# A Fourier layer and a gated feed-forward network in fp32 on one core: the first tile's down projection in plain form, and stored weights loaded from HBM by GpSimd's queue instead of SyncE's

## The chip, the cores and the metric

The kernel runs on one core of a Trainium2 chip. The metric is the device time of one execution in microseconds (us). The engines are named as in the profile: PE (TensorE, matmul), PEld (its weight loads, which overlap the matmuls), DVE (VectorE), ACT (ScalarE), POOL (GpSimd) and SP (SyncE, which here only issues DMAs; "SPq" is its DMA queue in the trace). PSUM is the memory that matmuls accumulate in, SBUF the memory of all other operands.

## What is computed

```python
def attention(x, w_r, w_i, b_r, b_i):            # x: 8 x 3008 x 256, float32
    X = np.fft.rfft(x, axis=1)
    Yr = X.real @ w_r - X.imag @ w_i + b_r
    Yi = X.real @ w_i + X.imag @ w_r + b_i
    Yr = np.sign(Yr) * np.maximum(np.abs(Yr) - 0.01, 0.0)
    Yi = np.sign(Yi) * np.maximum(np.abs(Yi) - 0.01, 0.0)
    return np.fft.irfft(Yr + 1j * Yi, n=3008, axis=1)

def moe(x, w_in, w_out):                          # 24064 x 256, 256 x 2048, 2048 x 256
    h = x @ w_in
    g = h * (1.0 / (1.0 + np.exp(-1.702 * h)))
    return g @ w_out
```

The result is `moe(attention(x))` with the batches laid end to end as 24064 tokens. `w_in` and `w_out` come as float64.

## The kernel before, in words

**Numbers.** A float32 product is made of three matmuls in the fast format fp32r (`mm3`, L136): each operand is split into a rounded part `hi` and the rest `lo`, and hi·hi, hi·lo and lo·hi are added up in PSUM. A split (`split`, L133; both lines show as L134 in the profile) is a cast on ACT, which makes `hi`, and a subtraction on DVE, which makes `lo`. The float64 weights are taken apart by integer operations (`from_float64`, L182 to L210): POOL issues the DMA of the raw words (`wraw`), ACT and DVE convert them.

**Two halves of the work.** The Fourier layer goes batch by batch. Stage A (tiles `xr`, `xh`, `aev`) contracts over 47, writes to DRAM, stage B (`br`, `kr`, `co`) contracts over 64, the mix (`mv`, then `yr` by four DMAs, L384) multiplies by the weights and applies the threshold, the inverse (`yh`, `iev`) writes `s2` to DRAM, and the last stage, `tokens`, reads that (`ur`) and fills a tile `y` of 1024 tokens for the network. The gated network goes tile by tile, 23.5 tiles of 1024 tokens, and each tile in 8 steps (q = 0 to 7) of 256 of the 2048 hidden columns. A program order written out in the main loop (L729 to L798) mixes the pieces of both; a scheduler then orders each engine's instructions from it.

**Up projection of a step.** It is a 2x2 block product done with seven products instead of eight (Strassen's scheme in Winograd's form, products 1 to 7, 3 matmuls each). It needs the weight blocks added up in a certain way, "turned". `turn_weights(0, q, ...)` (L226) does that for `w_in`. The turned weights come as two tiles, `wu` (4 products, 512 KB) and `wv` (3 products, 384 KB). The seven operands of the tile's tokens (`tk`) are split once for each tile.

**Down projection of a step.** Each step leaves four blocks of g, named (f, n). In steps 4 to 7 (`plain`, L625) a block is split (tile `gl`) and multiplied by two blocks of `wo_h` and `wo_l`, which stay in SBUF: 8 products, 24 matmuls. Steps 0 to 3 of each tile are "fast" (`NF = 4`, L32): their down projection uses the seven-product scheme too, with turned weights `wd` (4 products) and `we` (3 products). Four of the seven products are done at once (12 matmuls); the operands of the other three are kept in buffers `df` (12 of them) and multiplied in steps 4 to 7 (`solo`, L622, 9 matmuls), so that these have 33. Between the two, after step 3, `turn` (L506) combines the four PSUM banks of the tile: four copies on ACT, four additions on DVE. For a fast step `block` (L550) forms the operands with four additions and subtractions on DVE more (L564 to L572). The PSUM banks of the down projection are the tiles `po`, all others `pa`.

**Who casts g.** ACT casts blocks (0,0) and (0,1) and the fast operands; POOL casts (1,1) and (1,0) of the plain steps (`SPARE`, L461) and the three solo operands of steps 4 to 7 (`parts(..., True)`, L478).

**Turned weights in HBM.** They are made once, during tile 0, and written to HBM (`keep_turned`, L257, tiles `kept_u`, `kept_v`, `kept_d`, `kept_e`). All later tiles load them again: `load_turned` (L266) takes a new buffer and issues the load on SP's queue, 556 loads in the whole run. `wu` and `wd` share 4 buffers, `wv` and `we` another 4 (`WQ`). A load has to wait until PE has done with the buffer's old contents. A queue takes its DMAs in order, so what SP has behind it waits as well: the Fourier layer's loads and stores, all of which are on SP.

**At the start.** Before tile 0's first step three blocks of `w_in` and one of `w_out` are turned (`weights`, L671) and all four plain blocks of `w_out` are converted. During tile 0 the other five blocks of `w_in` and three of `w_out` are turned beside the steps (L731 to L734).

**What paces the mixture.** In each step a `pattern` (L761) says when the products of the up projection (numbers) and the products of the last step's down projection (0) are issued. `SHARE` (L636) spreads the Fourier pieces in `queue` over the 8 steps of a tile, in proportion; `p1` says by which step a batch must be through; `need` (L785) says how far `tokens` has to be in each step.

Of the kernel before, what the change touches and what calls it, by code (L numbers as in the profile page):

```python
# [110 lines left out]
def fourier_mix_then_gated_ffn(ctx: ExitStack, tc: tile.TileContext, x, w_r, w_i, b_r, b_i, w_in, w_out, pack, kbs, out):  # L111
# [20 lines left out]

    def split(hi, lo, src):  # L133
        return nc.scalar.copy(hi, src).ins, nc.vector.tensor_tensor(lo, src, hi.bitcast(F32), ALU.subtract).ins  # L134

# [78 lines left out]

    def plain_weights(q):
        a, e = from_float64(down_rows(q), False)
        hi, lo = wo_h[:, q - NF], wo_l[:, q - NF]
        nc.scalar.copy(hi, a)
        nc.vector.tensor_tensor(a, a, hi.bitcast(F32), ALU.subtract)
        nc.vector.tensor_tensor(lo, e, a, ALU.add)  # L220
# [5 lines left out]
    def turn_weights(d, q, spare):  # L226
# [22 lines left out]
        for h, t in zip(names, w):  # L249
            to = new_turned(0, h, q)  # L250
            split(to[:, 0], to[:, 1], t[:, :len(HALVES[h])])
            fresh.append((-1 if h == "e" else q + d, h, q, to))

# [3 lines left out]
    def keep_turned(n, behind):  # L257
        for item in [item for item in fresh if item[0] <= n]:
            fresh.remove(item)
            _, h, q, t = item  # L260
            with tc.issue_after(behind):
                nc.sync.dma_start(kept[h, q], flat(t))
            if h == "e":
                del turned_w[0, h, q]

    def load_turned(h, n):  # L266
        k, q = divmod(n, NQ)
        if k < NT and (k or h == "e") and q < (NF if h in "de" else NQ):
            nc.sync.dma_start(flat(new_turned(k, h, q)), kept[h, q])

# [189 lines left out]

    SPARE = ((1, 1), (1, 0))  # L461
    FACTORS = (1, 6, 2, 5, 7, 3, 4)
# [11 lines left out]
    def parts(t, w, name, tag, bufs, spare=False):  # L474
        p = buf([128, 2, TOK], F32R, name, tag=tag, bufs=bufs)
        hi, lo = p[:, 0, :w], p[:, 1, :w]
        if spare:
            nc.gpsimd.tensor_copy(hi, t)  # L478
            nc.vector.tensor_tensor(lo, t, hi.bitcast(F32), ALU.subtract)  # L479
        else:  # L480
            split(hi, lo, t)
        return hi, lo
# [46 lines left out]
    class Step:  # L529

        def __init__(self, tile, q, prev):


            self.tile, self.q, self.w, self.fast = tile, q, tile.w, q < NF
            self.b = prev.c if prev else None
            w = {h: turned_w.pop((tile.k, h, q)) for h in "uv"}
            self.wq = {p: (w[h][:, 0, i], w[h][:, 1, i]) for h in "uv" for i, p in enumerate(HALVES[h])}
            self.s, self.f, self.g = {}, {}, {}
# [8 lines left out]
        def cut(self, name, t):  # L547
            self.g[name] = parts(t, self.w, "gl", "gl", GL, name in SPARE)

# [58 lines left out]
        def down(self):  # L608
# [10 lines left out]

            we = turned_w.pop((tile.k, "e", q - NF))  # L620

# [3 lines left out]
            def plain(g, f, n, m):  # L625
                ms = slice(128 * m, 128 * m + 128)
                mm3(tile.bank(m, n), wo_h[:, q - NF, f, ms], wo_l[:, q - NF, f, ms], *g, start=False, stop=False, more=True)

            rest = [(lambda f=f, n=n: self.g[f, n], lambda g, f=f, n=n, m=m: plain(g, f, n, m)) for f, n in BLOCKS for m in range(2)]
            a, b, c = ((lambda t=t: parts(t, self.w, "gl", "gl", GL, True), lambda g, i=i, m=m, n=n: solo(g, i, m, n)) for i, (t, m, n) in enumerate(tile.solo.pop(0)))  # L630
            return rest[:1] + [a] + rest[1:3] + [b] + rest[3:5] + [c] + rest[5:]
# [3 lines left out]
    MANY = (6,0,2,0,5,0,7,0,0,3,0,0,0,4,0,1,0,0)  # L635
    SHARE = (1.6,.3,.3,.3,.5,1.6,1.7,1.7)  # L636

# [28 lines left out]
    def fill(count):  # L666
        for _ in range(2 * count):
            if filler:
                filler.pop(0)[1]()

    def weights(i):  # L671
        with ExitStack() as held_back:

            for ins in ([evacuated[11 if i == 1 else 15]] if i < 5 else mixed) if i else ():
                held_back.enter_context(tc.issue_after(ins))
            if i < 4:
                turn_weights(*((0, 0), (1, 0), (0, 1), (0, 2))[i], False)
                keep_turned(-1, stored[15])
            else:
                plain_weights(i + NF - 4)  # L680

# [18 lines left out]
    with tc.issue_after(loaded[2]), tc.issue_after(turned[-1]):  # L700
        fill(1)
    for i in range(4 + NQ - NF):
        weights(i)
# [134 lines left out]
```

## Time and profile before

| | |
|---|---|
| time before, median of 3 runs | 2605.38 us (2602.67 to 2610.48) |
| the profiled execution | 2605.41 us, of which its span is 2603.6 |
| PE busy | 2515.9 us, 97% |
| PEld busy | 2079.5 us, 80% |
| DVE busy | 1950.3 us, 75% |
| ACT busy | 1702.2 us, 65% |
| POOL busy | 385.5 us, 15% |
| moved by DMA | 466.17 MB, mean 179 GB/s |

The engines' busy times come from one profiled execution, whose own time stands in the second row. A group of instructions is given by source line, engine, operation and tiles, `out<-in`, with its count, its busy time, the mean length of one in ns, and the idle time of the engine just before them with what ended most of it. Matmuls overlap, so a matmul lasts longer in the record than the distance from one to the next.

### The profile page before, as it was taken

How to read it: one execution, taken by the hardware profiler on the slowest of the kernel's cores; microseconds unless marked ns; L12 is line 12 of the kernel's file. 1: busy time of each engine (PE TensorE's matmuls, PEld its weight loads, DVE VectorE, ACT ScalarE, POOL GpSimd, SP SyncE). 2: the span in 40 equal slices, each digit the busy share in tenths (PEclk: the TensorE clock that was granted, in tenths of full speed). 3: DMA queues.
4: the chain of work that ended last, by engine and by line, in shares of the span. 5: the costliest groups of instructions: out<-in, count | busy, mean ns of one | idle time of the engine just before them, and what ended most of it. 6: DMA issues, size and time to landing. Idle time of an engine off the chain costs nothing.

```text
span 2603.6 us, 37610 instructions
## 1 busy us (share of the span) xinstructions
PE 2515.9 (97%) x12477; PEld 2079.5 (80%) x12477; DVE 1950.3 (75%) x3173; ACT 1702.2 (65%) x3226; POOL 385.5 (15%) x508
## 2 busy tenths in 40 slices
PE   7889989999999999999999999999999999999998
PEld 4657878888788887888878888788887878888888
DVE  5787868778678786777867877678777787687776
ACT  4676757567676676666766767667577675675565
POOL 0002011210111111112121110110211111112212
PEclk8899999999999999999999999999999999999999
DMA  8686646455575555655566545656466564654455
GB/s 247 198 274 204 207 133 190 131 182 169 165 218 156 167 187 184 192 166 160 172 209 191 175 149 185 193 179 194 140 196 216 148 196 125 192 166 144 137 163 162
DMA packets 239938, 466.17 MB, mean 179 GB/s; under 512 B 28064, under 2 KB 115488, under 8 KB 239744
## 3 DMA queue, kind: packets, MB, share of 16 engines
q1 hardware_dynamic: 237312, 455.37, 56.1%
q0 software_dynamic: 2432, 8.39, 1.1%
q8 instruction: 100, 1.64, 0.3%
q14 instruction: 94, 0.77, 0.1%
HBM read 352.50 MB, written 85.98 MB: 168 GB/s over the span
## 4 chain that ended last, share of the span: by engine, by line
PE 79%; DMA 6%; DVE 4%; ACT 4%; issue 1%; SPq 1%; POOL 0%; ACTq 0%; DVEq 0%; POOLq 0%
PE pa L137 14%; PE pa L138 13%; PE pa L139 13%; PE po L137 11%; PE po L138 11%; PE po L139 11%; PE pa L449 4%; PE pa L349 2%; DMA yr<-mv 2%; DMA xr<-in_x 2%; ACT g L555 1%; DMA wu<-kept_u 1%; SPq L384 1%; PE pa L316 1%; DVE g L554 0%
## 5 line engine op out<-in xcount | busy, mean ns | idle before, releaser
L134 DVE TENSOR_TENSOR gl<-g,gl 128x512 fp32r<-128x512 f32 (+1 forms) x576 | 395.0, 696 | 150.1 <-ACT gl L134 148.2
L134 ACT CAST gl<-g 128x512 fp32r<-128x512 f32 (+1 forms) x576 | 350.3, 618 | 46.1 <-PE po L139 17.1
L478 POOL CAST gl<-df 128x512 fp32r<-128x512 f32 (+1 forms) x288 | 227.0, 790 | 746.4 <-PE po L139 711.4
L478 POOL CAST gl<-g 128x512 fp32r<-128x512 f32 (+1 forms) x192 | 146.5, 763 | 1287.4 <-ACT g L555 1008.8
L137 PE MATMUL pa<-tk,wu 128*128 128x512 f32 (+1 forms) x768 | 311.5, 406 | 22.0 <-ACT pa L582 9.6
L138 PE MATMUL pa<-tk,wu 128*128 128x512 f32 (+1 forms) x768 | 300.5, 391 | 0.0
L139 PE MATMUL pa<-tk,wu 128*128 128x512 f32 (+1 forms) x768 | 300.0, 391 | 0.0
L138 PE MATMUL po<-gl,wo_h 128*128 128x512 f32 (+1 forms) x768 | 298.4, 389 | 0.7 <-DVE gl L134 0.7
L545 ACT COPY s<-pa 128x512 f32<-128x512 f32 (+1 forms) x385 | 216.3, 584 | 122.0 <-PE pa L139 119.0
L139 PE MATMUL po<-gl,wo_l 128*128 128x512 f32 (+1 forms) x768 | 295.5, 386 | 0.0
L137 PE MATMUL po<-gl,wo_h 128*128 128x512 f32 (+1 forms) x768 | 289.3, 392 | 4.0 <-ACT gl L134 3.8
L554 DVE TENSOR_TENSOR g<-pa,s 128x512 f32<-128x512 f32 (+1 forms) x289 | 194.7, 675 | 86.3 <-PE pa L139 73.9
L555 ACT ACTIVATE g<-g 128x512 f32<-128x512 f32 (+1 forms) x289 | 179.7, 623 | 120.3 <-DVE g L554 117.9
L137 PE MATMUL pa<-tk,wv 128*128 128x512 f32 (+1 forms) x576 | 229.8, 399 | 0.7 <-ACT s L545 0.2
L479 DVE TENSOR_TENSOR gl<-df,gl 128x512 fp32r<-128x512 f32 (+1 forms) x288 | 208.3, 725 | 21.5 <-POOL gl L478 21.5
L138 PE MATMUL pa<-tk,wv 128*128 128x512 f32 (+1 forms) x576 | 222.5, 386 | 0.0
L139 PE MATMUL pa<-tk,wv 128*128 128x512 f32 (+1 forms) x576 | 222.2, 386 | 0.0
L137 PEld LDWEIGHTS pa<-tk,wu 128*128 128x128 f32 x768 | 146.7, 191 | 66.6 <-ACT pa L582 19.3
L555 ACT ACTIVATE g<-pa 128x512 f32<-128x512 f32 (+1 forms) x287 | 171.6, 598 | 28.0 <-PE pa L139 25.4
L139 PEld LDWEIGHTS pa<-tk,wu 128*128 128x128 f32 x768 | 146.3, 190 | 31.5 <-issue 0.8
L137 PEld LDWEIGHTS po<-gl,wo_h 128*128 128x128 f32 x768 | 143.3, 189 | 33.1 <-ACT gl L134 6.8
L138 PEld LDWEIGHTS pa<-tk,wu 128*128 128x128 f32 x768 | 146.8, 191 | 27.9 <-issue 1.9
(150 smaller groups left out, 5751.2 us busy)
## 6 DMA issues: line engine op xcount, KB each, us to landing
wu<-kept_u SPq DMA_DIRECT2D x184, 512.0 KB, 4.1
wv<-kept_v SPq DMA_DIRECT2D x184, 384.0 KB, 3.5
wd<-kept_d SPq DMA_DIRECT2D x92, 512.0 KB, 4.3
we<-kept_e SPq DMA_DIRECT2D x96, 384.0 KB, 3.6
s<-aev SPq DMA_DIRECT2D x128, 192.0 KB, 2.9
br<-s SPq DMA_DIRECT2D x96, 256.0 KB, 3.5
yr<-mv SPq DMA_DIRECT2D x384, 64.0 KB, 2.1
s<-iev SPq DMA_DIRECT2D x96, 256.0 KB, 2.6
```

Of the source, the lines that this page charges most:

```text
L134: return nc.scalar.copy(hi, src).ins, nc.vector.tensor_tensor(lo, src, hi.bitcast(F32), ALU.subtract).ins
L137: nc.tensor.matmul(ps, lhsT=wh, rhs=xh, start=start, stop=False, skip_group_check=more)
L138: nc.tensor.matmul(ps, lhsT=wh, rhs=xl, start=False, stop=False, skip_group_check=more)
L139: nc.tensor.matmul(ps, lhsT=wl, rhs=xh, start=False, stop=stop, skip_group_check=more)
L316: done_a.append(nc.tensor.matmul(ps[:96], lhsT=ka32, rhs=xs.pop(q), start=True, stop=True).ins)
L349: nc.tensor.matmul(pv[:, c, :, i], lhsT=t[:, i, cs], rhs=k[:, i], start=True, stop=True)
L449: turned.append(nc.tensor.matmul(pv[:, c, 94 * j:94 * j + 94], lhsT=t[:, j, 128 * c:128 * c + 128], rhs=kz, start=True, stop=True).ins)
L478: nc.gpsimd.tensor_copy(hi, t)
L479: nc.vector.tensor_tensor(lo, t, hi.bitcast(F32), ALU.subtract)
L545: nc.scalar.copy(t, ps[:, :self.w])
L554: nc.vector.tensor_tensor(t, ps[:, :w], self.s[other], ALU.add)
L555: nc.scalar.activation(t, ps[:, :w] if other is None else t, AF.Gelu_apprx_sigmoid)
```

## The change

It has these parts; each can be found in the diff by the names given.

- **Tile 0's steps 0 to 3 become plain** (`self.fast` asks for `tile.k > 0`). Blocks 0 to 3 of `w_out` are converted in plain form too (`wo_first`), into the `df` buffers, which tile 0 no longer uses for kept operands. `turn` and the solo products of tile 0 go.
- **The weights' conversions move.** The list `FIRST` has ten conversions ahead of the first step: (0, q) turns a block of `w_in`, (1, q) converts block q of `w_out` plainly; block 7 follows in step 0. `turn_weights(1, ...)`, four blocks, now runs in steps 2 to 5 of tile 0, and all of its results are written to HBM at once.
- **Loads on GpSimd's queue** (`load_turned`: `nc.gpsimd.dma_start`). Tile 0 loads nothing any more, so there are 552.
- **Casts.** ACT casts all blocks of g; POOL keeps the solo operands, and casts them by `tensor_scalar` (times 1, plus 0) instead of `tensor_copy`.
- **Pacing.** New `SHARE`, `p1` and `need`; the pattern of a step goes by how many down products are left from the step before (4, 8 or 11).

```diff
     def split(hi, lo, src, spare=False):
+        if spare:
+            cast = nc.gpsimd.tensor_scalar(hi, src, 1.0, 0.0, ALU.mult, ALU.add)
+        else:
+            cast = nc.scalar.copy(hi, src)
...
+    def plain_weights(q, spare):
+        a, e = from_float64(down_rows(q), spare)
+        if q < NF:
+            wo_first[q] = tuple(buf([128, 2, D], F32R, "wp", tag="df", bufs=DF) for _ in range(2))
+        hi, lo = wo_first[q] if q < NF else wo[q - NF]
...
-            fresh.append((-1 if h == "e" else q + d, h, q, to))
+            fresh.append((-1 if d else q, h, q, to))
...
-            if h == "e":
+            if h in "de":
                 del turned_w[0, h, q]
...
-        if k < NT and (k or h == "e") and q < (NF if h in "de" else NQ):
-            nc.sync.dma_start(flat(new_turned(k, h, q)), kept[h, q])
+        if 0 < k < NT and q < (NF if h in "de" else NQ):
+            nc.gpsimd.dma_start(flat(new_turned(k, h, q)), kept[h, q])
...
-    SPARE = ((1, 1), (1, 0))
...
-        if spare:
-            nc.gpsimd.tensor_copy(hi, t)
-            nc.vector.tensor_tensor(lo, t, hi.bitcast(F32), ALU.subtract)
-        else:
-            split(hi, lo, t)
+        split(hi, lo, t, spare)
...
-            self.tile, self.q, self.w, self.fast = tile, q, tile.w, q < NF
+            self.tile, self.q, self.w, self.fast = tile, q, tile.w, tile.k > 0 and q < NF
...
-            self.g[name] = parts(t, self.w, "gl", "gl", GL, name in SPARE)
+            self.g[name] = parts(t, self.w, "gl", "gl", GL)
...
-            we = turned_w.pop((tile.k, "e", q - NF))
+            wh, wl = wo_first.pop(q) if q < NF else wo[q - NF]
+            we = turned_w.pop((tile.k, "e", q - NF)) if tile.solo else None
...
+            if we is None:
+                return rest
...
+    MID = (6,0,2,0,5,0,7,0,3,0,1,0,4,0,0)
-    SHARE = (1.6,.3,.3,.3,.5,1.6,1.7,1.7)
+    SHARE = (1.3,.6,.6,.6,.6,1.3,1.5,1.5)
...
+    FIRST = ((0, 0), (1, 0), (0, 1), (0, 2), (1, 1), (1, 2), (1, 3), (1, 4), (1, 5), (1, 6))
...
-            if i < 4:
-                turn_weights(*((0, 0), (1, 0), (0, 1), (0, 2))[i], False)
-                keep_turned(-1, stored[15])
-            else:
-                plain_weights(i + NF - 4)
+            down, q = FIRST[i]
+            (plain_weights if down else lambda *at: turn_weights(0, *at))(q, False)
...
-        if n < NF - 1:
-            turn_weights(1, n + 1, True)
         if n < NQ - 3:
             turn_weights(0, n + 3, True)
+        if n + 7 < NQ:
+            plain_weights(n + 7, True)
+        if 2 <= n < NF + 2:
+            turn_weights(1, n - 2, True)
...
-            p1 = NQ * S * (nextb - 1) // TILE - 9
-        pattern = FEW if 1 <= q <= NF else MANY
+            p1 = NQ * S * (nextb - 1) // TILE - 11
+        pattern = {4: FEW, 8: MID, 11: MANY}.get(len(behind), MID)
...
-            need = TILE * (k + 1) + TILE * min(1.0, max(0.0, (part - NQ * k - 4) / 2.9))
+            need = TILE * (k + 1) + TILE * min(1.0, max(0.0, (part - NQ * k - 2) / 4.9))
...
-        if q == NF - 1:
+        if step.fast and q == NF - 1:
             closing = cur.turn
```

How this moves instructions shows at three places. Line numbers in the rows of the changed kernel are its own, four to nine higher than those of the kernel before. First DVE in tile 0's first step. Before, the sums (L554) and the fast operands (L564 to L572) stand between the `lo` parts of g (L134 with `gl`), with the turning of a block of weights (L242 and on) behind them:

```order
L554 TENSOR_TENSOR df<-pa,s 128x512
L554 TENSOR_TENSOR g<-pa,s 128x512
L564 TENSOR_TENSOR g<-g 128x512
L566 TENSOR_TENSOR g<-df,g 128x512
L568 TENSOR_TENSOR g<-g,df 128x512
L134 TENSOR_TENSOR gl<-g,gl 128x512
L572 TENSOR_TENSOR df<-g,df 128x512
L134 TENSOR_TENSOR wd<-wt,wd 128x512
L134 TENSOR_TENSOR gl<-g,gl 128x512
L242 TENSOR_TENSOR wt<-we,wa 128x128
```

The same place in the changed kernel (L558 are the sums, L138 with `gl` the `lo` parts of g, L229 the end of a plain block, L207 to L213 the conversion of the next float64 block):

```order
L558 TENSOR_TENSOR g<-pa,s 128x512
L229 TENSOR_TENSOR wo_l<-we,wa 128x512
L138 TENSOR_TENSOR gl<-g,gl 128x512
L558 TENSOR_TENSOR g<-pa,s 128x512
L207 TENSOR_SCALAR we<-we 128x512
L208 TENSOR_SCALAR wa<-we 128x512
L138 TENSOR_TENSOR gl<-g,gl 128x512
L210 SCALAR_TENSOR_TENSOR wa<-wraw,wa 128x256 x2
L212 TENSOR_SCALAR we<-wa 128x512
L213 TENSOR_TENSOR we<-we,wm 128x512
```

The fast operands are gone from it; the conversions stay between the `lo` parts. Second, SP's queue in a late, steady tile. Before, the loads of turned weights (L269) stand among the Fourier layer's DMAs (L384 `yr`, L441 `ur`, L333 and L334 for stage B):

```order
L384 DMA yr<-mv 64x256 x4
L441 DMA ur<-s_6673 96x512
L334 DMA br<-s_9867 128x2x256
L441 DMA ur<-s_6673 96x512
L333 DMA kr<-in_kbs 128x256
L269 DMA wd<-kept_d_100 128x1024
L269 DMA wv<-kept_v_92 128x768
L269 DMA we<-kept_e_107 128x768
L269 DMA wu<-kept_u_86 128x1024
L384 DMA yr<-mv 64x256 x4
```

In the changed kernel SP has the Fourier layer's DMAs alone:

```order
L393 DMA yr<-mv 64x256 x4
L450 DMA ur<-s_112 96x512
L343 DMA br<-s_6457 128x2x256
L342 DMA kr<-in_kbs 128x256
L393 DMA yr<-mv 64x256 x4
```

Third, POOL in a steady tile. Before, it has only casts, of the solo operands (`df`) and of blocks of g:

```order
L478 CAST gl<-df 128x512 x3
L478 CAST gl<-g 128x512 x2
L478 CAST gl<-df 128x512 x2
L478 CAST gl<-g 128x512
L478 CAST gl<-df 128x512
```

In the changed kernel the solo casts (L135) and the loads (L278) follow one another on POOL's in-order queue:

```order
L135 TENSOR_SCALAR gl<-df 128x512 x2
L278 DMA we<-kept_e_106 128x768
L135 TENSOR_SCALAR gl<-df 128x512
L278 DMA wd<-kept_d_100 128x1024
L278 DMA wv<-kept_v_92 128x768
L135 TENSOR_SCALAR gl<-df 128x512
L278 DMA we<-kept_e_107 128x768
L135 TENSOR_SCALAR gl<-df 128x512 x2
```

A solo cast now stands behind whatever load is ahead of it, with that load's wait for its buffer. POOL also has one row `L135 ISA` in the changed program, ahead of its first TENSOR_SCALAR.

More of the change, by code (lines that the diff above doesn't have):

```diff
@@ L131, in buf2, with split @@
         return buf([128, 2, D], F32, name, tag="w2", bufs=W2)
-    def split(hi, lo, src):
-        return nc.scalar.copy(hi, src).ins, nc.vector.tensor_tensor(lo, src, hi.bitcast(F32), ALU.subtract).ins
+    def split(hi, lo, src, spare=False):
+        if spare:
+            cast = nc.gpsimd.tensor_scalar(hi, src, 1.0, 0.0, ALU.mult, ALU.add)
+        else:
+            cast = nc.scalar.copy(hi, src)
+        return cast.ins, nc.vector.tensor_tensor(lo, src, hi.bitcast(F32), ALU.subtract).ins
     def mm3(ps, wh, wl, xh, xl, start=True, stop=True, more=False):
@@ L213, in down_rows @@
         return w_out[256 * q:256 * q + 256, :].rearrange("(f p) e -> p f e", p=128)
-    def plain_weights(q):
-        a, e = from_float64(down_rows(q), False)
-        hi, lo = wo_h[:, q - NF], wo_l[:, q - NF]
+    wo = [(wo_h[:, q], wo_l[:, q]) for q in range(NQ - NF)]
+    wo_first = {}
+    def plain_weights(q, spare):
[3 more added lines that the diff above has]
+        hi, lo = wo_first[q] if q < NF else wo[q - NF]
         nc.scalar.copy(hi, a)
@@ L626, in plain @@
                 ms = slice(128 * m, 128 * m + 128)
-                mm3(tile.bank(m, n), wo_h[:, q - NF, f, ms], wo_l[:, q - NF, f, ms], *g, start=False, stop=False, more=True)
+                mm3(tile.bank(m, n), wh[:, f, ms], wl[:, f, ms], *g, start=tile.k + q + f == 0, stop=False, more=True)
             rest = [(lambda f=f, n=n: self.g[f, n], lambda g, f=f, n=n, m=m: plain(g, f, n, m)) for f, n in BLOCKS for m in range(2)]
+            if we is None:
+                return rest
             a, b, c = ((lambda t=t: parts(t, self.w, "gl", "gl", GL, True), lambda g, i=i, m=m, n=n: solo(g, i, m, n)) for i, (t, m, n) in enumerate(tile.solo.pop(0)))
@@ L701, in fourier_mix_then_gated_ffn @@
         fill(1)
-    for i in range(4 + NQ - NF):
+    for i in range(len(FIRST)):
         weights(i)
```

## The prediction

> **What bounds the kernel now.** I read the page first, then the busy time by stretches, then the waits of PE and of SyncE's queue from the second tile on, and last the groups of instructions for prices. The page's first lines:
>
> ```profile
> span 2603.6 us, 37610 instructions
> PE 2515.9 (97%) x12477; PEld 2079.5 (80%) x12477; DVE 1950.3 (75%) x3173; ACT 1702.2 (65%) x3226; POOL 385.5 (15%) x508
> ```
>
> PE (TensorE) is the bound. The profiled execution took 2605.41 us, of which 1.8 lie outside its span; the median of the three runs is 2605.38, so the sum below stands for both. Of the 2603.6 us PE is idle for 87.7, and that, with the time at a lowered clock, is all that a change of order can win.
>
> The next fence is busy time by stretches: length, then PE, PEld, DVE, ACT, POOL busy (instructions), PE's granted clock, DMA share, GB/s. I cut at the first matmul of the gated network (122), the first `wo_h` product of tile 0 (217) and the first `wd` product of tile 1 (304).
>
> ```profile
> 0.00:122.00 122.00, 96.47 (x397) 70.28 (x397) 75.87 (x169) 61.10 (x119) 9.51 (x18) 0.89 0.77 231
> 122.00:217.00 95.00, 83.62 (x282) 52.38 (x281) 76.77 (x173) 71.30 (x145) 9.64 (x16) 0.89 0.76 251
> 217.00:304.00 87.00, 83.34 (x470) 70.61 (x469) 69.33 (x110) 55.11 (x99) 12.76 (x15) 1.00 0.62 194
> 304.00:400.00 96.00, 88.39 (x457) 74.55 (x456) 66.49 (x107) 57.14 (x107) 11.45 (x17) 0.95 0.49 151
> 400.00:2604.00 2204.00, 2164.11 (x10880) 1811.63 (x10878) 1661.79 (x2619) 1457.59 (x2758) 342.10 (x443) 1.00 0.56 174
> ```
>
> The second row holds tile 0's first four steps. There PE runs 282 matmuls in 95 us, against 470 in the 87 us behind, while DVE is 81% and ACT 75% busy: VectorE and ScalarE, which convert weights beside the steps' own work, hold PE back. PE idles for 95 - 83.6 = 11.4 us and loses 0.11 x 95 = 10.5 us to a lowered clock, 21.9 us at most in all. From 400 on PE idles 39.9 us in 2204, 1.8%.
>
> SyncE's own waits from 304 on (total, times, longest):
>
> ```profile
> SPq L269 <- PE pa L139: 669.4, 293, 10.0
> SPq L269 <- PE po L139: 396.9, 145, 9.1
> ```
>
> L269 is the load of the turned weights. Its queue stands still for 1066 us until PE gives a weight buffer back, and the Fourier stage's DMAs stand behind it. That would matter only as far as PE waits for those DMAs. PE's waits in the same stretch, its weight loads first and then its matmuls:
>
> ```profile
> PEld pa L137 <- ACT pa L582: 15.2, 20, 3.5
> PEld pa L137 <- ACT xh L134: 4.0, 6, 1.5
> PEld pa L137 <- ACT yh L394: 3.8, 1, 3.8
> PEld pa L137 <- DMA wu<-kept_u: 2.5, 1, 2.5
> ```
>
> ```profile
> PE pa L137 <- ACT pa L582: 7.5, 7, 3.0
> PE pa L449 <- DMA ur<-s: 4.1, 2, 2.3
> PE pa L137 <- DMA wu<-kept_u: 3.4, 3, 2.3
> PE pa L137 <- ACT yh L394: 3.3, 1, 3.3
> PE po L137 <- DMA wd<-kept_d: 2.3, 2, 2.0
> PE pa L137 <- ACT xh L134: 1.7, 3, 1.2
> ```
>
> ACT's xh and yh are themselves late because of DMAs, as ACT's waits from 400 on show:
>
> ```profile
> ACT yh L394 <- DMA yr<-mv: 60.3, 45, 3.4
> ACT xh L134 <- DMA xr<-in_x: 47.9, 35, 5.2
> ```
>
> So DMAs from behind the weight loads cost PE at most 4.1 + 4.0 + 1.7 + 3.8 + 3.3 = 16.9 us, and the weight loads themselves 8.2.
>
> **The change part by part.** Prices first, from the groups kept apart by shape:
>
> ```profile
> L203 DVE TENSOR_SCALAR we<-we 128x512 f32<-128x512 f32 x16 | 6.8, 422 | 24.1 <-ACT we L202 24.1
> L206 DVE SCALAR_TENSOR_TENSOR wa<-wraw,wa 128x256 int32<-128x256 int32 x16 | 6.0, 415 | 0.0
> L209 DVE TENSOR_TENSOR we<-we,wm 128x512 f32<-128x512 f32 x16 | 11.0, 685 | 0.5
> L241 DVE TENSOR_TENSOR wt<-we,wa 128x128 f32<-128x128 f32 x8 | 2.6, 322 | 0.1
> L248 DVE TENSOR_TENSOR wt<-wt 128x128 f32<-128x128 f32 x8 | 2.3, 283 | 0.0
> L134 DVE TENSOR_TENSOR wu<-wt,wu 128x512 fp32r<-128x512 f32 x5 | 3.4, 681 | 0.0
> L134 DVE TENSOR_TENSOR wv<-wt,wv 128x384 fp32r<-128x384 f32 x5 | 2.7, 549 | 0.0
> L572 DVE TENSOR_TENSOR df<-g,df 128x512 f32<-128x512 f32 x92 | 64.1, 697 | 1.4 <-ACT df L555 1.4
> ```
>
> Turning a block of weights costs DVE 3 x 0.42 + 2 x 0.42 + 0.69 + 8 x 0.30 + 0.68 + 0.55 = 6.4 us; a plain block 3 x 0.42 + 2 x 0.42 + 3 x 0.69 = 4.2 us.
>
> *Matmuls.* Plain steps take 24 matmuls for the down projection. The turned ones took 12 in steps 0 to 3 and 33 in steps 4 to 7. So 48 come to the first four steps, 36 leave the last four, 12 are new. Back to back they start 0.23 us apart:
>
> ```profile
> 140.76 0.39 PE L137 MATMUL pa<-tk,wu 128*128 128x512 f32 x1
> 140.99 0.39 PE L138 MATMUL pa<-tk,wu 128*128 128x512 f32 x1
> ```
>
> That is +11.0 us in steps 0 to 3 and -8.3 in steps 4 to 7, where PE is 96% busy and gives it back in full: **+2.7**.
>
> *DVE in tile 0.* In steps 0 to 3 the four sums of each step go (16 x 0.70 = 11.2), `turn`'s four additions go (2.8), and seven turned blocks become six and a plain one (6.4 - 4.2 = 2.2): 16.2 of 76.8 us. Nothing comes to ACT there. The stall is worth 21.9 us at most and nothing at least, since ACT at 75% keeps its share. I take two thirds, as DVE falls to about its steady share of 75%: **-14.6** (bounds -21.9 and 0). Steps 4 to 7 get two turned blocks (+12.8) and lose 12 subtractions of the solo operands (-8.4); 4.4 us more on a DVE that idles 18 of 87 there: 0, at worst +4.4.
>
> *Before the first step* there are three plain blocks more and a turned one less: 12.6 - 6.4 = 6.2 us of DVE. It has room until 100 and none between there and the first products: **+2** (0 to +6.2).
>
> *Casts of blocks (1,1) and (1,0)* go from POOL to ACT:
>
> ```profile
> L134 ACT CAST gl<-g 128x512 fp32r<-128x512 f32 x552 | 341.1, 627 | 43.8 <-PE po L139 15.2 <-issue 10.9 <-DVE g L564 9.3
> L478 POOL CAST gl<-g 128x512 fp32r<-128x512 f32 x184 | 142.7, 776 | 1269.7 <-ACT g L555 991.7 <-PE pa L139 124.0 <-PE pa L449 102.2
> ```
>
> 184 x 0.627 = 115 us, ACT 65% to 70%. PE's waits for ACT could grow with ACT's queue: the largest, on L582, is 22.7 us, and load over idle goes from 1.9 to 2.3, a fifth more on this and the like of it. Against that a cast is 0.15 us shorter and needs no hand-over to POOL: **+3** (-5 to +16).
>
> *Loads off SyncE.* The Fourier DMAs no longer stand behind them. Of the 16.9 us I take half, because a DMA that waits for its own producer gains nothing: **-8.5** (-16.9 to 0).
>
> *Loads on POOL.* What POOL's DMAs take to issue, and what transfers take to land (size, then median us):
>
> ```profile
> L200 POOL DMA_DIRECT2D wraw<-in_w_in x13 | 7.9, 609 | 68.7 <-DVE wt L248 42.6 <-DVE wa L206 16.2 <-DVE we L208 8.9
> ```
>
> ```profile
> wu<-kept_u SPq DMA_DIRECT2D x184, 512.0 KB, 4.1
> wd<-kept_d SPq DMA_DIRECT2D x92, 512.0 KB, 4.3
> xe<-in_x SPq DMA_DIRECT2D x8, 384.0 KB, 12.9
> wraw<-in_w_out POOLq DMA_DIRECT2D x5, 512.0 KB, 5.7
> wraw<-in_w_in POOLq DMA_DIRECT2D x3, 512.0 KB, 10.0
> ```
>
> Some 550 loads x 0.61 = 336 us of POOL, which is 15% busy. Landing lies between 4.3 and 10.0; the 10.0 were taken in the crowd of the start, when SyncE's own took 12.9, so I take 5.7, 1.4 us more than `wd` now. Six PE waits for `wu` and `wd` today, 1.4 more each: up to +8; I take **+3** (0 to +8), because the loads no longer queue behind SyncE's other work.
>
> *Solo casts* stay on POOL, now as TENSOR_SCALAR, behind loads. A load ahead costs its 0.61 us of issue, and its wait is for a matmul that lies earlier in PE's order than the cast's own buffer. The new form has no row on POOL: between DVE's 0.42 and twice POOL's 0.78 of today. I take 0.8. The library row that POOL executes once before the first of them is bounded by 0 and some us, beside PE work. **+3** (0 to +16).
>
> *The spread of the Fourier work* (`SHARE`, `need`, `p1`) moves pieces from steps 5 to 7 and 0 into steps 1 to 4. It can shrink the 39.9 us of idle or only move it: **-8** (-20 to +10).
>
> Sum: 2605.4 + 2.7 - 14.6 + 2 + 3 - 8.5 + 3 + 3 - 8 = **2588.0 us**.
>
> **The rivals.**
>
> *Order pays twice* (chance 0.17). If tile 0 gives the whole 21.9 and the spread takes half of the 39.9: 2588 - 7.3 - 12 = about 2568. For it: steady DVE and ACT are at 75% and 66%, so PE's waits are a matter of order. Against it: no single wait is large.
>
> *Nothing is gained* (0.15). The DMA waits turn out to be the transfers' own time, and ACT keeps tile 0's pace when DVE lets go: -14.6 and -8.5 become about -4 together, the spread 0, and with +2.7, +2, +3 and +3 + 3 it ends at about 2605 to 2615. For it: SyncE waits 1066 us and PE hardly notices. The Trainium skill has this as a rule ("DMA: Bandwidth & Descriptors", section "Issuing engines are not separate DMA queues"): all queues share the same 16 DMA engines, so another issuer saves sequencer time alone. By that the -8.5 would be 0 and the sum 2596.5; the trace differs in kind, as the 1066 us are waits for semaphores and not issue.
>
> *Loads land late* (0.12), the one that ends slower. A `wd` buffer comes free about one fast step ahead of its use. A fast step has 21 + 12 matmuls, 33 x 0.23 = 7.6 us, so beyond a landing of some 7.5 us each of the 92 `wd` loads stalls PE by the excess. At 8.0 us that is 92 x 0.5 = 46, and 2588 + 8.5 + 46 = about 2640. For it: the 10.0 row. Against it: the 5.7 row, from a time when DMAs were 70 to 80% busy. A page speaks for it too: "SBUF — State Buffer" of the Trainium skill, section "SBUF: two separate sides", says that a POOL-issued DMA starves while VectorE holds the shared port in its two-port form. The trace shows that form's price only in rows like L203, 0.42 us where L209 takes 0.69, and those end with the weight conversions.
>
> *Solo casts late* (0.06). If TENSOR_SCALAR takes 1.6 us, 276 casts come 0.8 later; should a quarter of them be needed at once, 69 x 0.8 = 55 us, about 2640.
>
> **How the numbers follow.** The forecast has 0.50, with 2578 to 2597 as its own range. A measurement of this kernel can tell 0.3% from no change, 2597.6 to 2613.2. Faster: 0.50 + 0.17 = 0.67. Same: 0.15. Slower: 0.12 + 0.06 = 0.18. The range goes down to 2556, as far as the first rival with its bounds, and up to 2620, which leaves out most of the last two rivals.
>
> **What would show it.** Right: tile 0's first four steps hold about 330 matmuls at a clock above 0.95, and tile 1's first `wd` product starts near 292 and not 304; no L269-like wait on SyncE, and PE's waits for `ur`, xh and yh at half; ACT busy about 1815 us; loads landing below 6.5 us. Wrong: `wd` or `wu` among PE's largest waits, POOL's `gl` in DVE's waits with more than 50 us, or ACT's L582 wait grown by more than half.

## The result and the profile after

The changed kernel takes 2631.4 us (median of 7 runs, 2618.96 to 2639.22) against 2605.38 (7 runs, 2601.85 to 2610.48): ratio 1.0093, 95% interval 1.0074 to 1.0111. I had forecast 2588, 0.7% faster. The profiled execution took 2637.12 us, 5.7 above the median. Its page begins:

```profile
span 2635.3 us, 37442 instructions
PE 2533.0 (96%) x12489; PEld 2086.3 (79%) x12489; DVE 1931.7 (73%) x3171; ACT 1799.2 (68%) x3430; POOL 532.6 (20%) x862
```

PE has 12 matmuls more, as worked out. It idles for 102.3 us (87.7 before), and its busy time is up by 17.1 us. Only 2.7 of these are the 12 matmuls. A matmul lasts 0.39 us in the record and the next can start 0.23 us after it, so a short wait leaves no gap and stands as busy time. The same stretches as before, columns as there:

```profile
122.00:217.00 95.00, 86.53 (x300) 54.20 (x299) 70.78 (x173) 65.87 (x139) 8.57 (x16) 0.92 0.69 227
217.00:304.00 87.00, 77.18 (x425) 64.94 (x426) 60.13 (x108) 56.34 (x107) 5.36 (x10) 0.96 0.61 193
304.00:400.00 96.00, 89.47 (x460) 74.37 (x461) 67.25 (x111) 62.64 (x118) 15.06 (x25) 0.98 0.54 167
400.00:2604.00 2204.00, 2153.99 (x10702) 1796.88 (x10701) 1644.87 (x2589) 1536.70 (x2903) 485.86 (x776) 0.99 0.55 173
```

From 400 on PE executes 10702 matmuls where it executed 10880, so most of the loss comes there; at 400 it is 33 matmuls behind (1573 against 1606). The stretch 217 to 304, which had PE 96% busy, now has 89%.

SyncE's queue no longer waits for weight buffers; it waits for its own producers instead (from 304 on):

```profile
SPq L393 <- DVE mv L386: 690.4, 73, 17.7
```

Who PE waits for from 304 on, its weight loads and then its matmuls:

```profile
PEld pa L141 <- ACT pa L586: 24.9, 29, 5.0
PEld pa L141 <- ACT s L549: 8.9, 16, 3.0
...
PEld po L141 <- DMA wd<-kept_d: 6.5, 4, 2.9
PEld pa L458 <- DMA ur<-s: 5.2, 3, 1.8
```

```profile
PE pa L141 <- ACT pa L586: 14.5, 14, 4.5
PE pa L458 <- DMA ur<-s: 7.3, 5, 2.6
PE po L141 <- DMA wd<-kept_d: 5.0, 3, 2.7
```

The wait for ACT's copy of product 1's bank (L582 before, L586 now) is up from 22.7 to 39.4 us; that for `ur` from 4.1 to 7.3 at the matmuls, with 5.2 at the weight loads besides; that for `wd` from 2.3 to 11.5 (6.5 and 5.0). xh is gone from the first rows. ACT itself waits longer for `yr` and shorter for `xr` (from 400 on):

```profile
ACT yh L403 <- DMA yr<-mv: 68.4, 53, 4.3
ACT xh L137 <- DMA xr<-in_x: 31.3, 25, 3.6
```

What the transfers take from issue to landing, of the kernel before and then of the changed one:

```profile
br<-s SPq DMA_DIRECT2D x96, 256.0 KB, 3.5
yr<-mv SPq DMA_DIRECT2D x384, 64.0 KB, 2.1
s<-iev SPq DMA_DIRECT2D x96, 256.0 KB, 2.6
ur<-s SPq DMA_DIRECT2D x128, 192.0 KB, 3.8
```

```profile
wu<-kept_u POOLq DMA_DIRECT2D x184, 512.0 KB, 4.3
...
wd<-kept_d POOLq DMA_DIRECT2D x92, 512.0 KB, 4.7
...
br<-s SPq DMA_DIRECT2D x96, 256.0 KB, 4.3
yr<-mv SPq DMA_DIRECT2D x384, 64.0 KB, 3.1
s<-iev SPq DMA_DIRECT2D x96, 256.0 KB, 3.3
ur<-s SPq DMA_DIRECT2D x128, 192.0 KB, 4.3
```

This is where the profile differs in kind. The loads that moved land 0.2 to 0.4 us later (`wu` 4.1 to 4.3, `wd` 4.3 to 4.7). The Fourier transfers, which did not move, land later: `yr` by half, `br`, `iev` and `ur` by 0.5 to 0.8 us.

One place shows how this can reach PE. ACT, SyncE and POOL of the changed kernel in order of time (start, length, what; in brackets idle time before it and what ended it), and then PE:

```profile
1722.05 0.59 ACT L549 COPY s<-pa 128x512 f32<-128x512 f32 x1 [0.52 <-PE pa L143]
1726.89 0.51 ACT L403 ACTIVATE yh<-yr,kc 128x256 fp32r<-128x256 f32 x1 [4.26 <-DMA yr<-mv]
...
1729.09 0.58 ACT L586 COPY pa<-pa 128x512 f32<-128x512 f32 x1
```

```profile
1721.92 2.39 SPq L393 DMA_DIRECT2D yr<-mv  x4
```

```profile
1722.31 0.53 POOL L278 DMA_DIRECT2D wu<-kept_u  x1 [6.72 <-PE pa L143]
1722.99 0.53 POOL L278 DMA_DIRECT2D wd<-kept_d  x1
```

```profile
1729.72 0.50 PE L141 MATMUL pa<-tk,wu 128*128 128x512 f32 x1 [4.54 <-ACT pa L586]
```

Two loads of 512 KB start between the four `yr` transfers. By the trace the `yr` issued ahead of them lands after 1.9 us, the other three after 4.4 to 6.7. ACT has yh next in its order and stands still for 4.26 us. The copy that PE waits for is the fourth instruction behind yh, and PE idles 4.54 us, though it does not read `yr` at all. One place shows how a late transfer reaches PE, not how much of the loss comes that way: with the loads on SP (a_loads_sp, below) ACT's longest wait for `yr` is 4.3 us as well.

### The profile page after: what moved, and what is told of

It is laid out like the page before. It is cut to its first block, busy times and chain, and to the rows that moved or that the text cites. A ratio compares the mean times of both kernels' runs of the same rounds, so it can differ in the third digit from the quotient of the medians.

```text
span 2635.3 us, 37442 instructions
## 1 busy us (share of the span) xinstructions
PE 2533.0 (96%) x12489; PEld 2086.3 (79%) x12489; DVE 1931.7 (73%) x3171; ACT 1799.2 (68%) x3430; POOL 532.6 (20%) x862
## 4 chain that ended last, share of the span: by engine, by line
PE 70%; DMA 11%; DVE 9%; ACT 5%; issue 2%; SPq 2%; POOL 0%; DVEq 0%; ACTq 0%; POOLq 0%
PE pa L141 11%; PE pa L142 11%; PE pa L143 11%; PE po L141 10%; PE po L142 10%; PE po L143 10%; DMA yr<-mv 5%; PE pa L458 3%; PE pa L358 3%; DVE gl L138 2%; SPq L393 1%; ACT g L559 1%; DMA ur<-s 1%; PE pa L377 1%; DMA xr<-in_x 1%
## 5 line engine op out<-in xcount | busy, mean ns | idle before, releaser
L138 DVE TENSOR_TENSOR gl<-g,gl 128x512 fp32r<-128x512 f32 (+1 forms) x768 | 523.6, 697 | 157.2 <-ACT gl L137 155.3
L137 ACT CAST gl<-g 128x512 fp32r<-128x512 f32 (+1 forms) x768 | 461.5, 617 | 63.0 <-PE po L143 35.5
L142 PE MATMUL po<-gl,wo_h 128*128 128x512 f32 (+1 forms) x768 | 297.8, 388 | 0.0
L141 PE MATMUL po<-gl,wo_h 128*128 128x512 f32 (+1 forms) x768 | 282.5, 389 | 3.7 <-ACT gl L137 3.0
L135 POOL TENSOR_SCALAR gl<-df 128x512 fp32r<-128x512 f32 (+1 forms) x276 | 210.1, 762 | 334.6 <-PE po L143 304.3
L558 DVE TENSOR_TENSOR g<-pa,s 128x512 f32<-128x512 f32 (+1 forms) x293 | 197.0, 676 | 75.5 <-PE pa L143 64.2
L138 DVE TENSOR_TENSOR gl<-df,gl 128x512 fp32r<-128x512 f32 (+1 forms) x276 | 190.9, 694 | 60.2 <-POOL gl L135 60.1
L278 POOL DMA_DIRECT2D wu<-kept_u x184 | 100.1, 544 | 620.9 <-PE pa L143 409.3
L278 POOL DMA_DIRECT2D wv<-kept_v x184 | 102.6, 558 | 521.4 <-PE pa L143 378.9
L141 PEld LDWEIGHTS pa<-tk,wu 128*128 128x128 f32 x768 | 146.5, 191 | 66.3 <-ACT pa L586 25.7
L143 PEld LDWEIGHTS pa<-tk,wu 128*128 128x128 f32 x768 | 146.7, 191 | 31.2 <-issue 0.5
```

The costliest lines, as they stand in the source:

```text
L135: cast = nc.gpsimd.tensor_scalar(hi, src, 1.0, 0.0, ALU.mult, ALU.add)
L137: cast = nc.scalar.copy(hi, src)
L138: return cast.ins, nc.vector.tensor_tensor(lo, src, hi.bitcast(F32), ALU.subtract).ins
L141: nc.tensor.matmul(ps, lhsT=wh, rhs=xh, start=start, stop=False, skip_group_check=more)
L142: nc.tensor.matmul(ps, lhsT=wh, rhs=xl, start=False, stop=False, skip_group_check=more)
L143: nc.tensor.matmul(ps, lhsT=wl, rhs=xh, start=False, stop=stop, skip_group_check=more)
```

## The experiments

Names that begin with b_ are the kernel before with something done, those with a_ the changed kernel with something undone or added. Ratios are to the kernel before on the same chip, where its median lay between 2605.4 and 2611.7 us, with 95% intervals; a difference between two of them carries both intervals, 0.2 to 0.3% in all. Theory A: the loads' own queue makes the Fourier transfers late. Theory B: the order that the scheduler makes for the new queue is the worse one. Theory C: it is POOL, which issues loads and casts. In these runs a changed queue brings a new order with it, so none of them separates A from B altogether.

### Each part alone

The edits are the change's own lines: the loads on `nc.gpsimd` (b_loads); `cut` without `SPARE` (b_casts); `SHARE`, `p1` and `need` (b_pace); and tile 0, its list `FIRST` and its patterns (b_tile0). The new form of the solo cast is in none of the four.

b_loads: 

> The kernel before with one part of the change alone: the 556 loads of turned weights go on GpSimd's queue, all else as before. Four parts can carry the change's +0.93% (about +24 us): the loads, the casts, tile 0, the pacing. If the loads carry it (Fourier transfers slower beside loads on a second queue: yr landing 2.1 to 3.1 us, br 3.5 to 4.3, ur 3.8 to 4.3, and POOL's in-order queue delaying wd and solo casts), this kernel takes 0.6 to 1.0% longer, 2621 to 2631, with yr landing near 3 us. If the casts on ACT carry it, this kernel is within 0.3% of before. If the recorded prediction's terms for this part hold (-8.5 and +3), it is about 0.2% faster, 2600.

b_casts: 

> The kernel before with one part alone: ACT casts blocks (1,1) and (1,0) of g, POOL only the solo operands. If ACT's longer queue carries the loss (PE's waits for the copy of product 1's bank rose from 22.7 to 32.4 us, for the copies s from 3.8 to 10.2, from 400 us on), this kernel takes 0.5 to 0.9% longer, 2618 to 2629. If the loads carry it, it is within 0.3%. The recorded prediction put +3 us on it, 0.1%.

b_pace: 

> The kernel before with one part alone: the new SHARE, p1 and need. If the spread of the Fourier work carries the loss, 0.4% or more longer, 2616 and up; the recorded prediction had -8 us, -0.3%, 2597; if the order of pieces hardly matters, within 0.2%.

b_tile0: 

> The kernel before with one part alone: tile 0 plain, with its conversions ahead of the first step and its patterns; loads on SP, casts of g on POOL by the old form, old pacing. Recorded terms: +2.7 for the matmuls, -14.6 for VectorE's relief, +2 for the start: about 2595, -0.4%. Against that, in the changed kernel's profile the time above back-to-back matmuls up to the end of tile 1 went from 88.4 to 94.5 us: if tile 0 is the cause of that, +6 + 2.7 = about 2614, +0.3%.

| part alone | median us | ratio | interval |
|---|---|---|---|
| b_loads | 2637.26 | 1.0104 | 1.0085 to 1.0122 |
| b_casts | 2608.13 | 0.9994 | 0.9980 to 1.0007 |
| b_pace | 2594.89 | 0.9944 | 0.9924 to 0.9964 |
| b_tile0 | 2607.93 | 0.9989 | 0.9975 to 1.0002 |

The loads alone cost as much as the whole change does (the intervals overlap). Pacing alone gains half of that, and the casts on ACT cost nothing. Tile 0 alone does in its first steps what I said, and gives it back later:

```profile
122.00:217.00 95.00, 88.64 (x330) 58.47 (x329) 76.20 (x180) 68.16 (x142) 16.29 (x26) 0.96 0.78 259
...
400.00:2604.00 2204.00, 2158.71 (x10831) 1807.22 (x10829) 1655.20 (x2609) 1451.63 (x2748) 339.00 (x441) 0.99 0.55 173
```

330 matmuls at a clock of 0.96 instead of 282 at 0.89; by 400 PE has done 1664 matmuls against 1606, and from there to 2604 it does 49 fewer, idle for 45.3 us where it was for 39.9.

### Undone, by halves, on another queue, and with ACT relieved

In a_loads_sp the loads are back on `nc.sync`, in b_loads_half only `wu` and `wv` are on `nc.gpsimd`, in b_loads_act all are on `nc.scalar`. b_loads_hold keeps ACT's yh out of the way:

```diff
+                with ExitStack() as held_back:
+                    if sp + 2 in copied:
+                        held_back.enter_context(tc.issue_after(copied[sp + 2]))
-                nc.scalar.mul(yh[:, i], y[:, i], f)
+                    nc.scalar.mul(yh[:, i], y[:, i], f)
```

a_loads_sp: 

> The changed kernel with one part undone: the loads of turned weights back on SP's queue. If the loads' queue is the cause (alone on the kernel before it cost 1.04%), and the other parts keep what they gave alone (pacing -0.56%, casts -0.06%, tile 0 -0.11%), this kernel is 0.5 to 0.8% faster than before, 2585 to 2593. If the loss comes from the parts meeting each other, it stays at or above before, 2605 or more. yr's landing (median 2.1 us before, 3.1 changed) should go back to 2.1.

b_loads_hold: 

> The kernel before with the loads on POOL's queue and one edit more: ACT's yh of a piece may only be issued behind the copy co two pieces further on. Theory A: ACT takes yh up at the time at which yr used to land, the transfer is 0.8 us later beside POOL's loads (mean of the fourth transfer 2.4 to 3.2 us), and ACT, which takes its work in order, holds up what PE waits for. Then holding yh back takes ACT's waits for yr (88 us of 2240) nearly away and gives back a good part of the 27 us: 2615 to 2625. Theory B: the loss is in the order that the scheduler makes, or spread over many transfers: 2630 or more, though ACT's waits for yr go.

b_loads_half: 

> The kernel before with two thirds of the loads on POOL's queue (wu and wv, 368) and the others (wd and we, 188) on SP's. If each load on the second queue costs its share, about 0.7% longer, 2624, with yr's landing between 2.1 and 2.4 us at the median. If it is POOL's loads of wd and we, which stand next to the solo casts in POOL's order, that cost: within 0.3% of before.

b_loads_act: 

> The kernel before with the loads on ACT's queue. For the transfers alone: if any second queue beside SP's makes yr land late, its median is 2.4 us or more here as well; if it is POOL's way of issuing, it stays at 2.1. The time says little, since ACT stands still at each load until PE gives the buffer back: I expect it longer by over 5%, above 2735.

| | median us | ratio | interval |
|---|---|---|---|
| a_loads_sp | 2594.56 | 0.9953 | 0.9940 to 0.9967 |
| b_loads_hold | 2625.33 | 1.0064 | 1.0050 to 1.0078 |
| b_loads_half | 2635.79 | 1.0111 | 1.0098 to 1.0124 |
| b_loads_act | 2608.58 | one run | |

Undoing the loads' queue turns the loss of 0.9% into a gain of 0.5%: it is the cause, though the gain is a little under the 0.5 to 0.8% that I expected. In a_loads_sp the landing of `yr` and PE's waits for ACT are back:

```profile
yr<-mv SPq DMA_DIRECT2D x384, 64.0 KB, 2.1
```

```profile
PEld pa L141 <- ACT pa L586: 10.0, 19, 1.3
...
PEld pa L141 <- ACT s L549: 5.2, 13, 0.7
```

PE's wait for `wd` is not back: 11.8 us in all (4.5 and 7.3) against 11.5, so it has no part in the loss. Holding yh back gave 0.4% of the 1.04, at the edge of what theory A expected. Two thirds of the loads cost as much as all of them, so the cost is not a share for each load. ACT's queue cost nothing in its one run, where I had expected 5%; `yr` landed at 2.2 us, between my two cases.

### POOL with nothing but loads; ACT's queue on the changed kernel; yh held with loads on SP

In a_solo_act and a_solo_act_sp the cast in `split` is `nc.scalar.copy` for all.

a_solo_act: 

> The changed kernel with the solo operands cast by ACT, so that POOL does nothing from tile 1 on but issue the loads. Beside it runs the same kernel with the loads on SP. Theory C: the loads cost because POOL has casts too: solo casts stand behind loads, and VectorE's instructions are drawn out while POOL issues and casts (DVE busy from 400 us on 1808 us in the changed kernel, 1776 with the loads on SP). Then this kernel and its partner are within 0.3% of each other. Theory A (later transfers beside POOL's loads, whatever else POOL does): this one is 0.7% or more longer than its partner, as the changed kernel is 1.4% longer than its own with loads on SP.

a_solo_act_sp: 

> The partner: the changed kernel with the solo operands cast by ACT and the loads on SP's queue. ACT gets 276 casts of 0.62 us, 171 us more, on 68%: 75% busy. If ACT at that share holds PE back, it is slower than 2595 by the same for both partners; VectorE loses the lengthening beside POOL's casts, 33 us from 400 us on. I expect 2590 to 2605.

a_loads_act: 

> The changed kernel with the loads on ACT's queue. On the kernel before that cost nothing (2608.6 beside 2608.2). If it holds here, it is as fast as with the loads on SP: 2590 to 2600, and the loss belongs to POOL's queue, not to a second queue. If ACT at 68% with loads that wait is too full, 2615 or more.

a_sp_hold: 

> The changed kernel with the loads on SP and ACT's yh held back behind the copy co two pieces on. ACT's waits for yr (37 us from 400 us on) should nearly go. If they cost PE as they did with the loads on POOL (11 us for 76 us of waits), 5 us less than 2594.6, about 2590; if they are slack of ACT, no difference.

| | median us | ratio | interval |
|---|---|---|---|
| a_solo_act | 2646.03 | 1.0140 | 1.0117 to 1.0164 |
| a_solo_act_sp | 2622.38 | 1.0038 | 1.0024 to 1.0051 |
| a_loads_act | 2623.56 | 1.0055 | 1.0033 to 1.0077 |
| a_sp_hold | 2592.21 | 0.9927 | 0.9911 to 0.9944 |

ACT at 74% costs 0.85% by itself (1.0038 to 0.9953), more than I had expected. With no cast left on POOL its loads still cost 1.0% (1.0140 to 1.0038), so theory C is not the whole of it. On the changed kernel ACT's queue costs 1.0% as well (1.0055 to 0.9953), unlike on the kernel before. Another queue, with the order that comes with it, is enough for a loss there; POOL is not needed.

### What yh carries, and yr alone in a second queue

a_hold and b_pace_hold have the edit of b_loads_hold; in a_sp_yr_pool the loads are on SP, and only `yr` is on `nc.gpsimd`.

a_hold: 

> The changed kernel, loads on POOL, with ACT's yh held back behind the copy co two pieces on. With the loads on SP the same kernel has a ratio of 0.993 to before. PE's idle time that goes back to a yr transfer is 30.8 us in the changed kernel and 13.7 with the loads on SP. Theory A: held back, the 17 us go, and what is left of the loss of 1.4% is about 0.6%: ratio 0.997 to 1.002. Theory B, or a loss spread over all transfers: ratio 1.006 or more.

b_loads_act_timed: 

> The kernel before with the loads on ACT's queue, the same as the one look before, now timed. If the one look holds, ratio 0.998 to 1.003, and POOL's queue is worse than ACT's by 1%. If a second queue costs as such, 1.004 or more.

a_sp_yr_pool: 

> The changed kernel with the loads on SP and only the four yr transfers of a piece on POOL's queue. For the transfers: if two queues side by side make yr late, the landing of yr rises above its median of 2.1 us although no load has moved, to 2.6 or more. If lateness came from POOL's loads alone, it stays near 2.1, or gets shorter, since no load stands ahead of it in its queue. Time: 0.3 to 1% above 2595, also because POOL waits for mv ahead of solo casts.

b_pace_hold: 

> The kernel before with the new pacing and yh held back: pacing alone gave a ratio of 0.9944. ACT's waits for yr there are about 40 us from 400 us on, and PE's idle time from yr 11.6 us. If holding back gives what it gave the changed kernel with loads on SP (0.9953 to 0.9927), the ratio is 0.990 to 0.993, the fastest so far; if nothing, 0.9944.

| | median us | ratio | interval |
|---|---|---|---|
| a_hold | 2624.57 | 1.0067 | 1.0046 to 1.0087 |
| b_loads_act_timed | 2606.81 | 0.9995 | 0.9982 to 1.0007 |
| a_sp_yr_pool | 2620.02 | 1.0048 | 1.0033 to 1.0063 |
| b_pace_hold | 2587.46 | 0.9923 | 0.9904 to 0.9941 |

Theory A as I had it, with ACT's wait for `yr` as the path, does not carry the whole loss. Held back, the changed kernel still loses 1.4% by the loads' queue (1.0067 to 0.9927), as it did unheld (1.0093 to 0.9953), which is what I had set for theory B or a loss spread over all transfers. Holding yh gains 0.2 to 0.3% with the loads on either queue. The edit did not take the wait away altogether, though. From 400 on, in a_hold and a_sp_hold:

```profile
ACT yh L406 <- DMA yr<-mv: 37.4, 27, 4.7
```

```profile
ACT yh L406 <- DMA yr<-mv: 17.5, 19, 1.9
```

The wait still grows by 20 us with the loads on POOL (26 unheld, 42.3 to 68.4), so this pair is a weak test. b_loads_hold is a stronger one: it has 22.2 us of this wait, the kernel before has 60.3, and it is still 0.6% slower. In a_sp_yr_pool no load has moved:

```profile
yr<-mv POOLq DMA_DIRECT2D x384, 64.0 KB, 3.6
```

```profile
ACT yh L403 <- DMA yr<-mv: 44.3, 42, 4.0
```

`yr` takes 3.6 us in a queue of its own where it took 2.1 in the one that it shared with the loads, and the kernel loses 1.0% (1.0048 to 0.9953). But ACT waits no longer for it than in a_loads_sp (44.3 us, 42.3 there). POOL's wait for mv ahead of its casts is in that 1.0% too, and so is POOL's own way of issuing in the 3.6 us.

On the kernel before, a pair speaks against the late landings as the cause. First b_loads_half, which loses 1.1%, then b_loads_act_timed, which loses nothing:

```profile
br<-s SPq DMA_DIRECT2D x96, 256.0 KB, 3.9
yr<-mv SPq DMA_DIRECT2D x384, 64.0 KB, 2.3
```

```profile
br<-s SPq DMA_DIRECT2D x96, 256.0 KB, 4.0
yr<-mv SPq DMA_DIRECT2D x384, 64.0 KB, 2.3
```

`ur` lands at 3.9 us in both. So there the landings are the same and the times differ by 1.1%.

### The kernel before with no casts on POOL

All casts in `parts` are on ACT; b_nopool_half has `wu` and `wv` on POOL's queue besides.

b_nopool: 

> The kernel before with all casts that POOL had (blocks (1,1) and (1,0) and the solo operands, 460) on ACT, loads on SP: the control of the pair. ACT goes from 65 to 76% busy, VectorE loses the lengthening beside POOL's casts. The changed kernel with loads on SP lost 0.85% by the same step for its solo operands alone, so I expect a ratio of 1.003 to 1.012.

b_nopool_half: 

> The same with wu and wv (368 loads) on POOL's queue, which does nothing else from tile 1 on. If VectorE's lengthening by POOL's issue and casts together is what cost 1.1% on the kernel before, it is gone here: within 0.3% of the control. If POOL's queue costs by its transfers or by the order that comes with it, this one is 0.7% or more longer than the control.

| | median us | ratio | interval |
|---|---|---|---|
| b_nopool | 2615.31 | 1.0039 | 1.0024 to 1.0054 |
| b_nopool_half | 2628.13 | 1.0092 | 1.0078 to 1.0106 |

The cost of the two thirds falls from 1.1% to 0.5%, between the two expectations: about half of it goes with POOL's casts, half stays. What goes shows on DVE. The engines' busy times of b_loads_half, b_loads_act_timed, b_nopool and b_nopool_half in turn, over the whole run:

```profile
PE 2530.0 (96%) x12477; PEld 2084.8 (79%) x12477; DVE 1965.2 (75%) x3173; ACT 1702.3 (65%) x3226; POOL 566.1 (21%) x876
```

```profile
PE 2519.3 (97%) x12477; PEld 2078.3 (80%) x12477; DVE 1944.3 (75%) x3173; ACT 1704.2 (65%) x3226; POOL 386.5 (15%) x508
```

```profile
PE 2520.4 (96%) x12477; PEld 2080.8 (80%) x12477; DVE 1889.8 (72%) x3173; ACT 1938.8 (74%) x3706; POOL 14.8 (1%) x28
```

```profile
PE 2529.0 (96%) x12477; PEld 2086.6 (79%) x12477; DVE 1889.1 (72%) x3173; ACT 1940.7 (74%) x3706; POOL 212.0 (8%) x396
```

DVE has the same 3173 instructions in all four and in the kernel before. With loads and casts on POOL they take 1965.2 us, 15 more than before the change (1950.3) and 21 more than with the loads on ACT. Without casts on POOL they take 60 us less, and the loads then add nothing (1889.8 and 1889.1). That this lengthening is what costs the half is argued from the two going together.

## Why the prediction was wrong

**The step that failed** is *Loads off SyncE* in the part-by-part sum: -8.5, bounded by -16.9 and 0. With *Loads on POOL* (+3) the move of the loads was put at -5.5. I had reasoned from who waits in the trace of before, and so only a gain or nothing could come of it. The runs show +27 us for the loads alone (1.0104) and 1.4% in the changed kernel. I priced the landing of the transfers that move, where 1.4 us more was too much (they land 0.2 to 0.4 later), and gave no price to what the loads would run beside: the transfers that stay, and DVE while POOL issues and casts. The bound at 0 had no reason behind it: no row showed two queues side by side for the steady part.

**SyncE's 1066 us** were of little cost. When the loads left, the waits for the Fourier DMAs did not shrink as a whole: ACT's for `xr` fell from 47.9 to 31.3 us, its waits for `yr` and PE's for `ur` rose. In the queue that waited for PE, loads and Fourier transfers stood one behind the other; side by side `yr` lands at 3.1 us instead of 2.1 in the changed kernel. That the order of one queue protects small transfers is only how I read this: with `wu` and `wv` on POOL and no casts there (b_nopool_half) `yr` still lands at 2.1.

**The rule of the Trainium skill** that I set beside this term ("DMA: Bandwidth & Descriptors", section "Issuing engines are not separate DMA queues"), that DMAs of all issuers run on the same 16 DMA engines, was the better guide: by it the term was 0. The trace agrees in that nothing was gained. A loss is not in that rule, and no run shows that the sharing is the reason for it.

**The other terms.**
- Matmuls: +12, as worked out.
- DVE in tile 0, with the matmuls and the start -9.9 in all (-14.6 + 2.7 + 2): alone -0.11% (-2.9 us, interval -6.5 to +0.5). The mechanism is right for b_tile0, 330 matmuls at 0.96; the gain was given back after 400, and that I had not allowed for. In the changed kernel it is 300 at 0.92. Two of my landmarks were misread: in the kernel before the first `wo_h` product starts at 204.7 us and tile 1's first `wd` product at 293.4, not at 217 and 304. So the second row reaches 12 us beyond the first `wo_h` product.
- Casts on ACT: +3 forecast, -1.6 measured, not to be told from 0.
- Solo casts: TENSOR_SCALAR takes what I took (0.8 us), where CAST took 0.776 on the blocks of g. What the term costs in time (+3) no run shows alone. The rows of the changed kernel, with the issue of a load (0.551 us, where I took 0.61):

```profile
L135 POOL TENSOR_SCALAR gl<-df 128x512 fp32r<-128x512 f32 x264 | 205.0, 778 | 324.8 <-PE po L143 294.5 <-DVE mv L383 11.7 <-DVE g L558 6.1
L278 POOL DMA_DIRECT2D wd<-kept_d x92 | 50.7, 551 | 285.0 <-PE pa L143 166.9 <-PE po L143 103.9 <-issue 6.2
```

- The spread: -8 forecast, -14.6 measured alone (-0.56%), within its bounds.

Put together the parts alone make +0.3%, and the change has +0.9%. So 0.6% comes from their meeting: the loads' queue costs 1.4% in the changed kernel and 1.0% alone, and the other parts together give 0.5% (a_loads_sp) where alone they add up to 0.7%.

**The rivals.** *Loads land late* had the right sign and the wrong transfers: `wd` lands at 4.7 us and not at 8, and PE waits 11.5 us for it in all, with the loads on SP 11.8. *Nothing is gained* named the sharing of DMA engines, as a gain of 0. None had a loss beside loads that land in time. Of the starving of POOL-issued DMAs beside VectorE, which the page "SBUF — State Buffer" of the Trainium skill has in "SBUF: two separate sides", the runs show nothing: `wu` lands in 4.3 us from POOL and in 4.1 from SP. They hardly test it, as the rows that I took for the two-port form (L203) end with the weight conversions. Most of the signs that I had set did work: ACT's L582 wait grew by 74%, POOL's `gl` stood in DVE's waits with 60.1 us (from 304 on), the first four steps had 300 matmuls instead of 330, and tile 1's first `wd` product started at 316.5. Three signs of being right came true all the same and told nothing: no wait for weight buffers on SyncE, ACT busy 1799 us, loads landing below 6.5.

**What stays open.** How the other queue costs 1.0 to 1.4% is not settled. Holding yh back gains 0.2 to 0.4%, with or without the second queue. On the kernel before, some half of the loss goes with POOL's casts. The rest is spread over PE's waits, of which those for L586 (39.4 us, 14.2 in a_loads_sp), s and `ur` are the largest that grow in the changed kernel.

The scheduler makes another order for each queue (theory B), and that was not tried apart. The orders do differ: of PE's 12489 matmuls 9185 stand at the same place in a_loads_sp and in the changed kernel, and 10805 of 12477 in the pair of b_nopool. Against it as the whole: six pairs of kernels that are alike but for loads on POOL (before with b_loads and with b_loads_half, a_loads_sp with the changed kernel, the pairs of a_solo_act, a_hold and b_nopool) lose 0.5 to 1.4%, and b_casts, with 8210 of 12477 matmuls at their old place, and b_tile0 are within 0.11% of before. For it: ACT's queue makes `yr` late on the kernel before too (2.3 us), at no cost.

The traces also show when the loss comes. The first `wd` product of tile 19, in the kernel before and in b_loads:

```profile
2222.32 0.39 PE L137 MATMUL po<-gl,wd 128*128 128x512 f32 x1
```

```profile
2253.11 0.39 PE L137 MATMUL po<-gl,wd 128*128 128x512 f32 x1
```

They are 30.8 us apart, and the ends of the spans 31.4. The last `yr` is issued at 2222.0 and 2252.3. So in the last 380 us, in which the loads and POOL's casts go on without the mix, hardly anything is added; at the rate until then it would be some 5 us. Over the six pairs what is added lies between -4.9 and +4.0, 0.3 on average, where the same rate would give about 4. This points at the meeting with the Fourier work, by its transfers or by its share of ACT and DVE, and not at the loads by themselves; it is one profiled execution for each kernel.

**The best version** is neither: b_pace_hold, the kernel before with the new pacing and yh held back, at 0.9923; a_sp_hold, the changed kernel with loads on SP and yh held back, is its equal at 0.9927.

## What to carry to other kernels

A queue's waits in a trace are no gain in themselves: before moving its transfers to another queue, ask what they will run beside, and give that a price, for the transfers that stay and for the engine that issues. A bound at 0 needs a row as much as any other. When a change has several parts, run each alone: here one part of +1.0% hid another of -0.6%. An in-order engine that takes up work at the moment when its data is due passes a delay on to whoever stands behind it; moving that work a little later in its order gave 0.2 to 0.4% in four kernels.

## What the runs showed of the hardware

- A 64 KB transfer between SBUF partitions (`yr`) lands in 2.1 to 2.3 us at the median in the queue that it shares with the loads. With loads and `yr` in different queues it takes 2.1 to 2.4 on the kernel before (2.1 in b_nopool_half, 2.3 with the loads on ACT, 2.4 on POOL) and 2.9 to 3.6 on the changed one (3.6 with `yr` alone moved).
- Loads on POOL and on ACT land about like those on SP: `wu` 4.2 to 4.5, 4.2, and 4.0 to 4.2 us.
- POOL's issue of a load takes 0.55 us, TENSOR_SCALAR on POOL 0.78 for 128x512 fp32, as its CAST does.
- DVE's instructions are drawn out while POOL casts: 480 casts on POOL make the same 3173 instructions take 1950.3 us instead of 1889.8, and loads issued beside the casts 1965.2 to 1967.6. Loads without casts do not (1889.1).
